# Second chunks of x2 turned by DMA in planes of 16-bit halves

## The chip, the cores and the metric

One core of one Trainium2 chip runs the whole program in one launch. The metric is the device time of an execution in microseconds. The kernel before takes 731.89 us, the median of three executions (731.84 to 732.41).

## The reference, cut to what matters

Four batches of 448 positions and 768 channels go through sigmoid attention, a gated convolution block and a token and channel mixer. The stretch that matters here is the output projection and the token mixing behind it:

```
x  = attn(q, k, v)                       # (4, 448, 768)
g  = sigmoid(causal_conv5(x))
x2 = (g * (x @ w_val)) @ w_out           # the x2 of this document
u  = x2 + (relu(x2.T @ w_tok1) @ w_tok2).T
out = u + relu(u @ w_ch1) @ w_ch2
```

`x2` is computed with its channels on the partitions (x2.T), and `x2.T @ w_tok1` contracts over positions, so it needs x2 with positions on the partitions: each 128 x 448 chunk has to be turned over.

## The kernel before, in words

Weights and inputs are kept as pairs of a rounded high part and a low remainder, and each product is three matmuls (high x high, low x high, high x low). The work runs in stages: attention for all batches, then for each batch `b` the steps that `dense_steps(b)` hands back, then the channel mixer (`ch1`, `ch2`), which is two thirds of the time that is left.

The steps of a batch are called on TensorE in a list order written by hand. `val` holds six value projections (`proj(0, j)`, 18 matmuls each), whose result VectorE multiplies into the gate (L343) and splits into a high and a low part (L86 on ScalarE, L92 on VectorE). `outs` holds six output projections (`proj(1, j)`, 18 matmuls each, j is the chunk of 128 channels), whose result ScalarE copies to `x2T[j]` (L348), the transposes of the chunks (`transp(j)`, four 128 x 128 transposes on TensorE, L357, with a high part by ScalarE, L359, and a low part by VectorE, L360 and L361), and the token mixer: `tok1(half, t)` (11 matmuls of 384 columns, L374, needs three chunks of one half) and `tok2(j)` (6 matmuls, L387, whose sum VectorE adds to `x2T`, L391, and POOL stores). The second half's `tok1` and its `tok2` are called within the next batch's `val`, as `back1` and `back2`. The last 64 positions of a chunk are held twice (L349), so that the fourth transpose has 128 columns.

Beside these steps other work is woven in by `weave`, which calls a list of small operations in proportion to the matmuls passed. Within `outs` of batch b it is the convolution of batch b+1 (`post_ops`): six items, each of five passes of VectorE (L302 and four of L304), a high part by ScalarE (L309), a low part by VectorE (L312), a sigmoid by ScalarE (L315), and the load of a later item (`x_back`). Within `val` of batches 1 and 2 it is the decoding of three channel-mixer weights (`ch_ops`, `decode_ops`): six pieces `raw` of 768 KB are loaded by the SP queue (`ld_ch`), worked on by six passes of VectorE and two of ScalarE, and stored again by POOL (`keep`, L602). There are two buffers `raw`, and the load of piece n+2 is called behind the eighth operation of piece n:

```
                if k == 7:
                    load(n + 2)
```

Each engine and each queue works through its own instructions strictly in the order in which the program calls them. PSUM tiles of these steps come from one pool of six.

Of the kernel before, what the change touches and what calls it, by code (L numbers as in the profile page):

```python
# [30 lines left out]
def tile_kernel(ctx, tc, qT, kT, v, w_val, conv_w, w_out, w_tok1, w_tok2, w_ch1, w_ch2, out):  # L31
# [130 lines left out]
    dn = {}  # L162
    pd = {}

    wt1H = wts.tile([P, NF + 1, NTOK], F32R, name="wt1H")
# [153 lines left out]
    def dense_steps(b):  # L319
        gv, x2T, x2, h1 = {}, {}, {}, {}  # L320
        cur = {}

        def proj(sel, j, part):
# [16 lines left out]
            if sel == 0:  # L340
                g = gate_t.pop(b * NP + j)

                nc.vector.tensor_tensor(out=g, in0=ps[:, :S], in1=g, op=ALU.mult)  # L343
                gv[j] = mid.tile([P, 2, S], F32R, tag="g", bufs=6, name="gv")
                split(gv[j][:, 0], gv[j][:, 1], g)
            else:
                x2T[j] = dn["late"].tile([P, 512], F32, tag="x2T", bufs=KD, name="x2T")
                nc.scalar.activation(out=x2T[j][:, :S], in_=ps[:, :S], func=AF.Copy)  # L348
                nc.vector.tensor_copy(x2T[j][:, S:], x2T[j][:, R0:S])  # L349

        def transp(j):
            half, jj = divmod(j, KH)
            if jj == 0:
                x2[half] = dn["late"].tile([P, 2 * NF + 1, HALF], F32R, tag="x2", bufs=1, name="x2")
            pt = pd["pool"].tile([P, NF + 1, P], F32, tag="d", bufs=pd["n"], name="pst")
            for c in range(NF + 1):
                nc.tensor.transpose(pt[:, c], x2T[j][:, c * P : (c + 1) * P], ident)  # L357
            x = x2[half][:, :, jj * P : (jj + 1) * P]
            nc.scalar.activation(out=x[:, : NF + 1], in_=pt, func=AF.Copy)  # L359
            nc.vector.tensor_tensor(out=x[:, NF + 1 :], in0=pt[:, :NF], in1=f(x[:, :NF]), op=ALU.subtract)  # L360
            nc.vector.tensor_tensor(  # L361
                out=x[REM:, NF], in0=pt[REM:, NF], in1=f(x[REM:, NF]), op=ALU.subtract
            )

# [51 lines left out]
        if b == 0:  # L416

            first[2:4] = first[3], first[2]
        outs = first + tr(0) + pj(1, 2) + tr(1) + pj(1, 3) + tr(2) + pj(1, 4)
        outs += t1(0, 0) + t1(0, 1) + pj(1, 5) + tr(3) + t2(0) + tr(4) + t2(1) + tr(5) + t2(2)  # L420
        return val, outs, t1(1, 0) + t1(1, 1), t2(3) + t2(4) + t2(5)

# [152 lines left out]
    def ld_ch(pool, fc, which):  # L575
        raw = pool.tile([P, 2 * DC], I32, tag="raw", bufs=2, name="raw")
        if which == 0:
# [47 lines left out]
    def ch_ops(pool, pieces):  # L625
# [5 lines left out]

        load(0)
        load(1)
        ops = []
        for n in range(len(pieces)):
            cur = []

            def op(k, n=n, cur=cur):
# [3 lines left out]
                if k == 7:  # L642
                    load(n + 2)

# [60 lines left out]
    with tc.manual_schedule():  # L705
# [23 lines left out]
        for b in range(B):  # L729
# [4 lines left out]
            else:  # L734
# [101 lines left out]
```

## Time and profile before

| | |
|---|---|
| median of three executions | 731.89 us |
| the profiled execution | 731.72 us, span 729.8 us |
| TensorE busy | 724.2 us of the span (99%) |
| VectorE busy | 398.9 us (55%) |
| ScalarE busy | 256.7 us (35%) |
| POOL busy | 40.2 us (6%) |
| granted clock of TensorE | full in all 40 slices |
| transposes of x2 (L357) | 96 in 24 groups of four |

The page gives first each engine's busy time, then its share in 40 equal slices, then the DMA queues, the chain of waits that ended last, and groups of instructions. The three stretches from one batch's first output projection to the next one's are alike; a stretch of time is read best from the timeline, which lists an engine's instructions in order with the idle time ahead of each.

### The profile page before, as it was taken

To read this page: it belongs to the slowest core of one execution; us is meant where nothing else is said; L and a number is where in the kernel's file an instruction comes from. 1 tells how busy PE (TensorE), PEld (TensorE's weight loads), DVE (VectorE), ACT (ScalarE), POOL (GpSimd) and SP (SyncE) were. 2 spreads that over 40 slices of the span, in tenths; PEclk is the share of its full clock that TensorE was granted. 3 is DMA by queue.
4 is the path that set the end of the run, shared out by engine and by line. 5 is a ranking of instruction groups with operands and counts; after the bars stand their busy time and mean duration, and the time that the engine had idled before them with its cause. 6 is when DMAs were issued, how large, how long until landed. Compare 5 with 4: busy or idle time off the path is not lost.

```text
span 729.8 us, 10824 instructions
## 1 busy us (share of the span) xinstructions
PE 724.2 (99%) x4360; PEld 594.1 (81%) x4360; DVE 398.9 (55%) x690; ACT 256.7 (35%) x379; POOL 40.2 (6%) x90
## 2 busy tenths in 40 slices
PE   8999999999999999999999999999999999999998
PEld 3344444799999999999998888888888899999997
DVE  1899766489889878965577999320100400040002
ACT  6899888344334333422343434200000200020000
POOL 0001100000111111002012000000000000000000
PEclk9999999999999999999999999999999999999999
DMA  9847997221344232044927453250000610042001
GB/s 298 252 153 236 266 299 234 83 91 47 102 150 147 76 127 101 17 147 131 311 82 227 162 172 127 67 172 0 1 0 1 201 38 0 1 128 67 1 1 65
DMA packets 56737, 87.24 MB, mean 120 GB/s; under 512 B 8032, under 2 KB 48240, under 8 KB 56688
## 3 DMA queue, kind: packets, MB, share of 16 engines
q1 hardware_dynamic: 50352, 62.86, 28.1%
q0 software_dynamic: 5904, 23.23, 9.0%
q8 instruction: 34, 0.56, 0.3%
q10 hardware_dynamic: 432, 0.46, 0.2%
q14 instruction: 15, 0.12, 0.1%
HBM read 66.68 MB, written 19.86 MB: 119 GB/s over the span
## 4 chain that ended last, share of the span: by engine, by line
PE 98%; ACT 1%; DVE 1%; issue 0%; ACTq 0%
PE psd L334 24%; PE psh L674 24%; PE pso L695 24%; PE pss L256 8%; PE psy L271 8%; PE pst L374 4%; PE pst L387 4%; PE pst L357 1%; ACT ga L258 1%; PE psi L718 0%; DVE dec_a L123 0%; DVE w L132 0%; ACT dec_a L111 0%; DVE dec_e L129 0%; DVE ur L701 0%
## 5 line engine op out<-in xcount | busy, mean ns | idle before, releaser
L88 DVE SCALAR_TENSOR_TENSOR r<-psh,r 128x384 fp32r<-128x384 f32 (+1 forms) x47 | 29.3, 623 | 213.4 <-ACT r L86 213.4
L674 PE MATMUL psh<-us,wch 128*128 128x512 f32 (+1 forms) x648 | 135.5, 362 | 0.0
L695 PE MATMUL pso<-r,wch 128*128 128x384 f32 (+1 forms) x630 | 131.1, 361 | 0.0
L674 PEld LDWEIGHTS psh<-us,wch 128*128 128x128 f32 x648 | 117.3, 188 | 12.7
L695 PEld LDWEIGHTS pso<-r,wch 128*128 128x128 f32 x630 | 113.8, 188 | 11.9
L86 ACT ACTIVATE r<-psh 128x384 fp32r<-128x384 f32 (+1 forms) x47 | 25.5, 543 | 230.7 <-PE psh L674 230.6
L334 PE MATMUL psd<-gv,wo 128*128 128x448 f32 x432 | 92.3, 369 | 0.0
L258 ACT ACTIVATE ga<-pss,bias_s 128x896 f32<-128x896 f32 x84 | 83.6, 1005 | 19.0 <-PE pss L256 18.2
L334 PE MATMUL psd<-xs,w 128*128 128x448 f32 x432 | 89.9, 367 | 0.0
L334 PEld LDWEIGHTS psd<-xs,w 128*128 128x128 f32 x432 | 80.9, 188 | 8.2 <-issue 0.7
L334 PEld LDWEIGHTS psd<-gv,wo 128*128 128x128 f32 x432 | 80.2, 188 | 6.6
L256 PE MATMUL pss<-q,k 64*64 64x448 f32 x672 | 78.5, 537 | 1.0 <-ACT ga L258 0.9
L271 PE MATMUL psy<-ga,v 64*64 64x448 f32 x672 | 77.6, 536 | 0.0
L304 DVE SCALAR_TENSOR_TENSOR gate<-xb,cw,gate 128x448 f32<-128x448 f32 x96 | 65.7, 685 | 2.8
L256 PEld LDWEIGHTS pss<-q,k 64*64 64x64 f32 x672 | 26.0, 133 | 39.4 <-issue 29.0
L271 PEld LDWEIGHTS psy<-ga,v 64*64 64x64 f32 x672 | 25.7, 133 | 37.4 <-issue 35.9
L111 ACT ACTIVATE dec_a<-dec_a,exp_b 128x768 int32<-128x768 int32 (+3 forms) x43 | 36.8, 868 | 37.1 <-DVE dec_a L108 37.1
L123 DVE SCALAR_TENSOR_TENSOR dec_a<-raw,dec_a 128x768 int32<-128x768 int32 (+2 forms) x42 | 37.3, 888 | 19.7 <-ACT dec_a L111 19.7
L674 PE MATMUL psh<-us,w 128*128 128x512 f32 (+1 forms) x216 | 45.2, 362 | 0.0
L695 PE MATMUL pso<-r,w 128*128 128x512 f32 (+1 forms) x216 | 45.1, 362 | 0.0
L674 PEld LDWEIGHTS psh<-us,w 128*128 128x128 f32 x216 | 39.1, 188 | 4.3
L695 PEld LDWEIGHTS pso<-r,w 128*128 128x128 f32 x216 | 39.1, 188 | 4.2
(80 smaller groups left out, 648.7 us busy)
## 6 DMA issues: line engine op xcount, KB each, us to landing
raw<-w_ch SPq DMA_DIRECT2D x24, 768.0 KB, 4.4
v<-v SPq DMA_DIRECT2D x24, 224.0 KB, 6.5
uscr<-x2T POOLq DMA_DIRECT2D x24, 224.0 KB, 3.7
q<-qT SPq DMA_DIRECT2D x23, 224.0 KB, 4.3
k<-kT SPq DMA_DIRECT2D x22, 224.0 KB, 4.5
raw<-w_out POOLq DMA_DIRECT2D x6, 768.0 KB, 8.4
wscr<-pre POOLq DMA_DIRECT2D x12, 384.0 KB, 3.6
xscr<-xb SPq DMA_DIRECT2D x18, 224.0 KB, 4.7
```

What stands on the lines that cost most here:

```text
L88: nc.vector.scalar_tensor_tensor(out=l_out, in0=src, scalar=0.0, in1=f(h_out), op0=ALU.max, op1=ALU.subtract)
L111: nc.scalar.activation(out=t["a"], in_=t["a"], func=AF.Relu, scale=8.0, bias=exp_b)
L123: nc.vector.scalar_tensor_tensor(out=t["a"], in0=hi, scalar=-0x80000000, in1=t["a"], op0=ALU.bitwise_and, op1=ALU.bitwise_or)
L256: nc.tensor.matmul(ps[cols, j, :S], k[rows, keys], q[rows], start=True, stop=True)
L258: nc.scalar.activation(out=a, in_=ps[:, :, :S], func=AF.Sigmoid, bias=bias_s, scale=QK_SCALE)
L271: nc.tensor.matmul(y_t[i + h][cols, :S], v_t[i][rows, c, cols], a[rows, j], start=c == 0, stop=c == NB - 1)
L304: nc.vector.scalar_tensor_tensor(out=acc, in0=x[:, t : t + S], scalar=w, in1=acc, op0=ALU.mult, op1=ALU.add)
L334: nc.tensor.matmul(ps[:, :S], w(a, kk), s[:, c, :], start=kk == 0 and n == 0, stop=kk == KD - 1 and n == 2,)
L374: nc.tensor.matmul(ps[:, :HALF], a, x[:, m], start=n == 0, stop=n == len(mm) - 1)
L387: nc.tensor.matmul(ps[:, :S], a, m[:, t, :], start=t == 0 and n == 0, stop=t == KT - 1 and n == 2)
L674: nc.tensor.matmul(ps[:, :n_t], wch[fc][0][a][:, kk * P : (kk + 1) * P], us_t[t, kk][:, c, :], start=kk == 0 and n == 0, stop=kk == KD - 1 ...
L695: nc.tensor.matmul(acc[j][:, :n_t], wch[fc][1][a][:, j * P : (j + 1) * P], r[c], start=fc == 0 and n == 0, stop=fc == KF - 1 and n == 2,)
```

## The change

In batches 0, 1 and 2 the chunks 0, 2 and 4 no longer go to TensorE. Behind the copy of `x2T[j]` ScalarE writes the low and the high 16 bits of each word into two planes (`planes`: one pass over 2 x 448 halves, one over the 2 x 64 that are held twice), and the SP queue turns the 128 x 1024 halves by one DMA transpose into `planesT`. Later (`joined`) ScalarE puts the halves together into words (one pass over 1024 halves), writes the high part (one pass over 512 words), and VectorE the low part in two passes, as before. `planes`, `planesT` and `word` have one buffer each. VectorE's copy of the 64 positions (L349) falls away for these chunks.

The list of `outs` is written in another order for batches 0 to 2: the first joining stands behind projection 2, the second behind projection 4, and `tok1` of the first half behind projection 5 where it stood behind projection 4. The decoding of the stored weights has one buffer `raw` where it had two, so the load of piece n+1 is called behind the eighth operation of piece n.

```diff
@@ dense_steps
                 x2T[j] = dn["late"].tile([P, 512], F32, tag="x2T", bufs=KD, name="x2T")
                 nc.scalar.activation(out=x2T[j][:, :S], in_=ps[:, :S], func=AF.Copy)
-                nc.vector.tensor_copy(x2T[j][:, S:], x2T[j][:, R0:S])
+                if by_dma(j):
+                    planes(j)
+                else:
+                    nc.vector.tensor_copy(x2T[j][:, S:], x2T[j][:, R0:S])
+        def by_dma(j):
+            return b + 1 < B and j % 2 == 0
...
+        def planes(j):
+            p = tp["pool"].tile([P, 2, 512], U16, tag="planes", bufs=1, name="planes")
+            w = x2T[j].bitcast(U16).rearrange("p (n t) -> p t n", t=2)
+            nc.scalar.activation(out=p[:, :, :S], in_=w[:, :, :S], func=AF.Copy)
+            nc.scalar.activation(out=p[:, :, S:], in_=w[:, :, R0:S], func=AF.Copy)
+            pt = tp["pool"].tile([P, 2, NF + 1, P], U16, tag="planesT", bufs=1, name="planesT")
+            nc.sync.dma_start_transpose(pt.rearrange("p t c d -> p (t c) d"), p.rearrange("p t n -> p (t n)"))
+            pl[j] = pt
+        def joined(j):
...
+            w = tp["pool"].tile([P, NF + 1, P], F32, tag="word", bufs=1, name="word")
+            nc.scalar.activation(
+                out=w.rearrange("p c d -> p (c d)").bitcast(U16).rearrange("p (n t) -> p t n", t=2),
+                in_=pl.pop(j).rearrange("p t c d -> p t (c d)"), func=AF.Copy,
+            )
+            x = x2[half][:, :, jj * P : (jj + 1) * P]
+            nc.scalar.activation(out=x[:, : NF + 1], in_=w, func=AF.Copy)
+            nc.vector.tensor_tensor(out=x[:, NF + 1 :], in0=w[:, :NF], in1=f(x[:, :NF]), op=ALU.subtract)
+            nc.vector.tensor_tensor(
+                out=x[REM:, NF], in0=w[REM:, NF], in1=f(x[REM:, NF]), op=ALU.subtract
+            )
...
+        def jn(j):
+            return [(0, lambda: joined(j))]
...
-        outs = first + tr(0) + pj(1, 2) + tr(1) + pj(1, 3) + tr(2) + pj(1, 4)
-        outs += t1(0, 0) + t1(0, 1) + pj(1, 5) + tr(3) + t2(0) + tr(4) + t2(1) + tr(5) + t2(2)
+        if b + 1 < B:
+            tr0, tr2, tr4 = jn(0), jn(2), jn(4)
+        outs = first + pj(1, 2) + tr0 + tr(1) + pj(1, 3) + pj(1, 4) + tr2 + pj(1, 5) + t1(0, 0) + t1(0, 1)
+        outs += tr(3) + tr4 + t2(0) + t2(1) + tr(5) + t2(2)
@@ ld_ch
-        raw = pool.tile([P, 2 * DC], I32, tag="raw", bufs=2, name="raw")
+        raw = pool.tile([P, 2 * DC], I32, tag="raw", bufs=1 if fc in PRE else 2, name="raw")
@@ ch_ops
-        load(0)
-        load(1)
+        held = 1 if pieces[0][0] in PRE else 2
+        for n in range(held):
+            load(n)
...
                 if k == 7:
-                    load(n + 2)
+                    load(n + held)
```

The changed program's order shows three places. The first is ScalarE in `outs` of batch 1, around projections 1 to 4. Names: `xs` is an item's high part, `gate` its sigmoid, `x_...` the turned chunk's high part. Before:

```order
L348 ACTIVATE x2T<-psd 128x448
L315 ACTIVATE gate<-gate 128x448
L359 ACTIVATE x_2408<-pst 128x4x128
L309 ACTIVATE xs<-xb 128x448
L348 ACTIVATE x2T<-psd 128x448
L315 ACTIVATE gate<-gate 128x448
L359 ACTIVATE x_2408<-pst 128x4x128
L309 ACTIVATE xs<-xb 128x448
L348 ACTIVATE x2T<-psd 128x448
```

Now, from the copy of chunk 2:

```order
L350 ACTIVATE x2T<-psd 128x448
L378 ACTIVATE planes<-x2T 128x2x448
L379 ACTIVATE planes<-x2T 128x2x64
L317 ACTIVATE gate<-gate 128x448
L389 ACTIVATE word<-planesT 128x2x512
L394 ACTIVATE x_2454<-word 128x4x128
L368 ACTIVATE x_2454<-pst 128x4x128
L311 ACTIVATE xs<-xb 128x448
L350 ACTIVATE x2T<-psd 128x448
```

The first joining (L389, L394, of chunk 0) stands behind the planes of chunk 2, and the high part of chunk 1 (L368) behind both.

The second place is VectorE in the same stretch, up to the low part of the last chunk that `tok1` waits for. Before, from the low part of chunk 1 to that of chunk 2:

```order
L360 TENSOR_TENSOR x_2408<-pst,x_2408 128x3x128
L361 TENSOR_TENSOR x_2408<-pst,x_2408 64x128
L304 SCALAR_TENSOR_TENSOR gate<-xb,cw,gate 128x448 x2
L312 TENSOR_TENSOR xs<-xb,xs 128x448
L302 TENSOR_SCALAR gate<-xb,cw 128x448
L304 SCALAR_TENSOR_TENSOR gate<-xb,cw,gate 128x448
L349 COPY x2T<-x2T 128x64
L304 SCALAR_TENSOR_TENSOR gate<-xb,cw,gate 128x448
L360 TENSOR_TENSOR x_2408<-pst,x_2408 128x3x128
```

Now, from the low part of chunk 1 (L369, L370), which follows that of chunk 0 (L395, L396) at once, to that of chunk 2 (the last row):

```order
L369 TENSOR_TENSOR x_2454<-pst,x_2454 128x3x128
L370 TENSOR_TENSOR x_2454<-pst,x_2454 64x128
L306 SCALAR_TENSOR_TENSOR gate<-xb,cw,gate 128x448 x2
L314 TENSOR_TENSOR xs<-xb,xs 128x448
L304 TENSOR_SCALAR gate<-xb,cw 128x448
L306 SCALAR_TENSOR_TENSOR gate<-xb,cw,gate 128x448
L354 COPY x2T<-x2T 128x64
L306 SCALAR_TENSOR_TENSOR gate<-xb,cw,gate 128x448 x3
L314 TENSOR_TENSOR xs<-xb,xs 128x448
L304 TENSOR_SCALAR gate<-xb,cw 128x448
L306 SCALAR_TENSOR_TENSOR gate<-xb,cw,gate 128x448 x2
L395 TENSOR_TENSOR x_2454<-word,x_2454 128x3x128
```

Between the low parts of chunks 1 and 2 stood six passes and a copy of VectorE; now it is eleven passes and a copy.

The third place is VectorE behind that, up to the low parts of `tok1`'s two results (`h_...`), which `tok2` waits for. Now:

```order
L396 TENSOR_TENSOR x_2454<-word,x_2454 64x128
L306 SCALAR_TENSOR_TENSOR gate<-xb,cw,gate 128x448 x2
L314 TENSOR_TENSOR xs<-xb,xs 128x448
L354 COPY x2T<-x2T 128x64
L304 TENSOR_SCALAR gate<-xb,cw 128x448
L306 SCALAR_TENSOR_TENSOR gate<-xb,cw,gate 128x448
L89 SCALAR_TENSOR_TENSOR h_2592<-pst_2580,h_2592 128x384
L306 SCALAR_TENSOR_TENSOR gate<-xb,cw,gate 128x448 x2
L89 SCALAR_TENSOR_TENSOR h_2610<-pst_2598,h_2610 128x384
```

Before it read:

```order
L361 TENSOR_TENSOR x_2408<-pst,x_2408 64x128
L304 SCALAR_TENSOR_TENSOR gate<-xb,cw,gate 128x448 x2
L312 TENSOR_TENSOR xs<-xb,xs 128x448
L302 TENSOR_SCALAR gate<-xb,cw 128x448
L349 COPY x2T<-x2T 128x64
L304 SCALAR_TENSOR_TENSOR gate<-xb,cw,gate 128x448 x2
L88 SCALAR_TENSOR_TENSOR h_2548<-pst_2536,h_2548 128x384
L304 SCALAR_TENSOR_TENSOR gate<-xb,cw,gate 128x448 x2
L88 SCALAR_TENSOR_TENSOR h_2566<-pst_2554,h_2566 128x384
```

The passes between the last low part and those of `tok1`'s results are nearly the same as before; all of them stand one convolution item further back.

## Rows read from the trace of the kernel before

**Rows 1.** The page, part 1: busy us, share, instructions.

```profile
PE 724.2 (99%) x4360; PEld 594.1 (81%) x4360; DVE 398.9 (55%) x690; ACT 256.7 (35%) x379; POOL 40.2 (6%) x90
```

**Rows 2.** Windows, batches 1 and 0: us, busy us of PE PEld DVE ACT POOL, clock.

```profile
216.74:278.75 62.01, 62.01 (x321) 57.36 (x320) 52.35 (x95) 22.62 (x40) 7.70 (x18) 1.00 0.33 109
...
154.72:216.74 62.02, 62.02 (x322) 57.27 (x321) 53.41 (x97) 24.28 (x43) 4.88 (x13) 1.00 0.34 110
```

**Rows 3.** Timeline, TensorE, batch 1: start, us, line, what, count.

```profile
278.75 7.60 PE L334 MATMUL psd<-gv,wo 128*128 128x448 f32 x36
286.19 0.60 PE L357 MATMUL pst<-ident,x2T 128*128 128x128 f32 x4
...
290.28 0.60 PE L357 MATMUL pst<-ident,x2T 128*128 128x128 f32 x4
...
298.45 0.34 PE L374 MATMUL pst<-x,wt1H 128*128 128x384 f32 x1
...
302.29 3.87 PE L334 MATMUL psd<-gv,wo 128*128 128x448 f32 x18
```

**Rows 4.** Timeline, ScalarE, the same batch.

```profile
282.67 0.55 ACT L348 ACTIVATE x2T<-psd 128x448 f32<-128x448 f32 x1 [4.58 <-PE psd L334]
...
290.92 0.57 ACT L315 ACTIVATE gate<-gate 128x448 f32<-128x448 f32 x1
291.39 0.59 ACT L359 ACTIVATE x<-pst 128x512 fp32r<-128x512 f32 x1
```

**Rows 5.** Groups by line, shapes apart, ScalarE: busy us, mean ns | idle.

```profile
L111 ACT ACTIVATE dec_a<-dec_a,exp_b 128x768 int32<-128x768 int32 x36 | 33.7, 936 | 37.1 <-DVE dec_a L108 37.1
...
L111 ACT ACTIVATE dec_a<-dec_a,exp_b 128x256 int32<-128x256 int32 x4 | 2.0, 498 | 0.0
```

**Rows 6.** Timeline, VectorE, the same batch.

```profile
276.92 0.63 DVE L92 TENSOR_TENSOR gv<-gate,gv 128x448 fp32r<-128x448 f32 x1 [0.65 <-ACT gv L86]
...
280.40 0.45 DVE L302 TENSOR_SCALAR gate<-xb,cw 128x448 f32<-128x448 f32 x1
280.88 1.40 DVE L304 SCALAR_TENSOR_TENSOR gate<-xb,cw,gate 128x448 f32<-128x448 f32 x2
...
287.93 0.56 DVE L360 TENSOR_TENSOR x<-pst,x 128x384 fp32r<-128x384 f32 x1
288.50 0.29 DVE L361 TENSOR_TENSOR x<-pst,x 64x128 fp32r<-64x128 f32 x1
288.82 0.68 DVE L304 SCALAR_TENSOR_TENSOR gate<-xb,cw,gate 128x448 f32<-128x448 f32 x1
289.43 0.62 DVE L312 TENSOR_TENSOR xs<-xb,xs 128x448 fp32r<-128x448 f32 x1
289.96 0.45 DVE L302 TENSOR_SCALAR gate<-xb,cw 128x448 f32<-128x448 f32 x1
```

**Rows 7.** Timeline, VectorE, batch 0: its first convolution pass.

```profile
158.79 0.45 DVE L302 TENSOR_SCALAR gate<-xb,cw 128x448 f32<-128x448 f32 x1
```

**Rows 8.** Timeline, VectorE, value projections of batch 1: pieces' last and first passes.

```profile
196.56 0.96 DVE L132 SCALAR_TENSOR_TENSOR pre<-raw,dec_e 128x768 fp32r<-128x768 f32 x1
...
200.15 0.55 DVE L108 TENSOR_SCALAR dec_a<-raw 128x768 int32<-128x768 int32 x1
...
205.47 0.96 DVE L132 SCALAR_TENSOR_TENSOR pre<-raw,dec_e 128x768 fp32r<-128x768 f32 x1
...
208.35 0.56 DVE L108 TENSOR_SCALAR dec_a<-raw 128x768 int32<-128x768 int32 x1
209.49 0.62 DVE L343 TENSOR_TENSOR gate<-psd,gate 128x448 f32<-128x448 f32 x1 [0.59 <-PE psd L334]
```

**Rows 9.** DMA issues from 160 to 330 us: count, KB each, us to landing.

```profile
raw<-w_ch SPq DMA_DIRECT2D x6, 768.0 KB, 5.2
...
xb<-xscr SPq DMA_DIRECT2D x14, 224.0 KB, 2.5
```

**Rows 10.** DMA issues of the whole span: the slowest kind.

```profile
w<-wscr POOLq DMA_DIRECT2D x8, 384.0 KB, 8.9
```

More of the change, by code (lines that the diff above doesn't have):

```diff
@@ L13 @@
 U32 = mybir.dt.uint32
+U16 = mybir.dt.uint16
 AF = mybir.ActivationFunctionType
@@ L163, in tile_kernel @@
     pd = {}
+    tp = {}
     wt1H = wts.tile([P, NF + 1, NTOK], F32R, name="wt1H")
@@ L319, in dense_steps @@
     def dense_steps(b):
-        gv, x2T, x2, h1 = {}, {}, {}, {}
+        gv, x2T, x2, h1, pl = {}, {}, {}, {}, {}
         cur = {}
@@ L348, in proj @@
                 nc.scalar.activation(out=x2T[j][:, :S], in_=ps[:, :S], func=AF.Copy)
-                nc.vector.tensor_copy(x2T[j][:, S:], x2T[j][:, R0:S])
+                if by_dma(j):
[4 more added lines that the diff above has]
+            return b + 1 < B and j % 2 == 0
         def transp(j):
             half, jj = divmod(j, KH)
-            if jj == 0:
+            if half not in x2:
                 x2[half] = dn["late"].tile([P, 2 * NF + 1, HALF], F32R, tag="x2", bufs=1, name="x2")
@@ L362, in transp @@
                 out=x[REM:, NF], in0=pt[REM:, NF], in1=f(x[REM:, NF]), op=ALU.subtract
+            )
[8 more added lines that the diff above has]
+        def joined(j):
+            half, jj = divmod(j, KH)
+            if half not in x2:
+                x2[half] = dn["late"].tile([P, 2 * NF + 1, HALF], F32R, tag="x2", bufs=1, name="x2")
+            w = tp["pool"].tile([P, NF + 1, P], F32, tag="word", bufs=1, name="word")
[8 more added lines that the diff above has]
+                out=x[REM:, NF], in0=w[REM:, NF], in1=f(x[REM:, NF]), op=ALU.subtract
             )
@@ L741, in tile_kernel @@
                 dn["late"] = tc.alloc_tile_pool(name="late", bufs=1, side="right", reuse_waits="tile")
+                tp["pool"] = tc.alloc_tile_pool(name="tp", bufs=1, side="left")
                 pre = tc.alloc_tile_pool(name="pre", bufs=1, side="left")
@@ L751, in tile_kernel @@
                 pre.release()
+                tp["pool"].release()
                 xbp.release()
```

## The prediction

> **What bounds the kernel now.** I read the page's busy times first: TensorE is busy for 99% of the span, no other engine above 55% [rows 1]. So time can only be won by taking matmuls away, and anything that makes TensorE wait is lost in full. The windows then show that each stretch from one batch's first output projection to the next one's takes 62.0 us, with TensorE busy throughout at full clock, and VectorE busy for 52 to 53 us of it [rows 2]. VectorE is thus the next engine in line, and its idle time is not spread evenly: within `outs` it runs almost without a gap. The timelines give the pace of each kind of step, and the order shows what stands behind what.
>
> **What is removed.** In TensorE's timeline two projections of 18 take 286.19 - 278.75 = 7.44 us, 3.72 each, or 0.207 a matmul; a projection with a group of four transposes takes 290.28 - 286.19 = 4.09, so the group costs 0.37; two `tok1` take 302.29 - 298.45 = 3.84, 1.92 each and 0.175 a matmul [rows 3]. Three groups a batch go, in three batches: 9 x 0.37 = **-3.3 us**. That is all that can be won.
>
> **What is added on ScalarE.** No row shows a pass over 16-bit elements. The nearest are the integer passes: 0.936 us for 768 elements, 0.498 for 256, so 0.86 ns an element [rows 5]. That gives 1.05 us for 896 halves, 0.39 for 128 and 1.16 for 1024; a next pass starts about 0.1 before the end of one it doesn't need (0.57 long, 0.47 apart [rows 4]). As bounds I take half of that, if halves go at twice the pace, and 1.6 times, if the step of two halves costs more. ScalarE has the time for it (24 of 62 us [rows 2]); the place matters. Times from here on run from a batch's first output projection.
>
> Projection 2 ends at 3 x 3.72 = 11.16. The copy `x2T` starts 0.20 later (282.47 to 282.67) and takes 0.55 [rows 3, 4]: 11.9. Planes of chunk 2: 13.25. A sigmoid: 13.7. Only then does the joining of chunk 0 stand in ScalarE's queue: the word to 14.8, the high part (0.59 [rows 4]) to **15.4**.
>
> **Who waits for that.** VectorE's queue has chunk 0's low part behind two items of convolution and half a third. An item takes 3.75: L302 0.48, four L304 at 0.71 (0.61 if the next doesn't need it), L312 0.53 [rows 6]. In batch 0 it begins at 158.79 - 154.72 = 4.07 [rows 2, 7] and reaches that low part at 13.5, so VectorE stands still until 15.4. From there to the last low part that `tok1` needs (chunk 2) the order has (L306, L314, L354, L395 and the like are lines of the changed kernel, for L304, L312, L349, L360): two low parts, 2 x 0.90 (L360 0.57, L361 0.33 apart), two L306 1.33, L314 0.53, L304 0.48, L306 0.61, a copy 0.1, three L306 2.04, L314 0.53, L304 0.48, two L306 1.33 [rows 6]. The sum is 9.2: it starts at 24.6 and ends at 25.15. ScalarE has its high part long before that: copy 4 ends at 18.96 + 0.36 + 0.75 = 19.7, planes 21.1, word 22.2, high part 22.8.
>
> TensorE wants it at the third matmul of `tok1`: six projections 22.32, one group of transposes 0.37, two matmuls 0.35: 23.05. It waits **2.1 us**. Then the rest of `tok1` (28.7), a group of transposes (29.1) and four matmuls of `tok2` bring it to 29.9, where it needs the low part of `tok1`'s second result. VectorE has in between L396 0.33, two L306 1.33, L314 0.53, a copy 0.1, L304 0.48, L306 0.61, L89 0.47, two L306 1.33, L89 0.56 (L360 taken for L89 [rows 6]): 25.15 + 5.75 = 30.9. It waits **1.05 us** more. A batch is then 62.0 - 1.1 + 2.1 + 1.05 = 64.05, that is **+6.1 us** over three, with the -3.3 in it.
>
> **One buffer raw.** The load of the next piece can go out only when VectorE's last pass on this one has ended; 768 KB land after 5.2 us [rows 9]. VectorE came to the next piece 200.15 - 197.52 = 2.6 us later at the first border and 208.35 - 206.43 = 1.9 at the second [rows 8]. It will stand 2.6 and 3.3 us there, less 0.6 that it waited for TensorE anyway [rows 8]: 5.3 late at the end of `val`, in batches 1 and 2. The low part of the last gated value ended at 277.55, 1.2 ahead of `outs` [rows 3, 6], and now ends at 4.1; projection 0 needs it at 17 x 0.207 = 3.5. So 4.7 is covered and 0.6 is lost. Item 0 began at 1.65 [rows 3, 6] and now at 6.95; the 64-position copy of chunk 1, behind it and half of item 1, is done at 12.6, and the one group of transposes wants it at 11.16 + 0.6: 0.85 lost. VectorE comes to the joining at 16.3, 0.3 behind the word, while TensorE's need at `tok1` lies 0.85 later, so 0.55 of the wait of 2.1 is used up: +0.9, twice, **+1.8**. If loads land in 4.2 the cover holds and this is nothing; at 6.4 it is 2 to 3 us a batch.
>
> **The transposing DMA.** No row shows one. Its 256 KB lie between 2.5 us (224 KB by the same queue [rows 9]) and 8.9 (the slowest kind [rows 10]). I take the load's 5.2, since the two share the queue. What does a duration T cost? Chunk 0's planes are done at 3.72 + 0.75 + 1.35 = 5.9; its transfer must free the one buffer `planes` before chunk 2's passes, and chunk 2's transfer must wait for the first word (1.35 + 0.45 + 1.15), then planes of chunk 4, word, high part, low part (3.8): 12.65 + 2T. That passes 25.15 only from T = 6.2 on. Below it the transfer costs nothing; above, 2 us a batch for each us of T. At 8.9: 30.45, 5.3 later, +16 us in all. In the SP queue the loads of items behind a transposing transfer wait with it; they are wanted some 10 us later and land in 2.5 [rows 9].
>
> The Trainium skill speaks against the change here: VectorE: DVE Perf Modes, section The three transpose paths, has 1.3 us for 128 x 128 through the crossbar against 0.39 on TensorE, and its table sends a transpose to TensorE where PSUM will do. Eight such blocks one after another would be 10.5 us (an estimate from that page), and by the formula +25.5 us more, 765 us. Advanced Engine Details and Errata, section X-Bar Transpose (TRN2), has such transfers as fast as plain ones, and by that T stays off the path. No run so far shows which.
>
> **Sum.** 731.72 (profiled execution) + 6.1 + 1.8 = 739.6. That execution lies 0.17 under the median, so 739.8 is compared with 731.89. A difference of 0.2% (1.5 us) is about what can be told from none.
>
> **The rivals.**
> - **Long transfers.** Above T = 6.2 the two transfers in a row set the end, each with the loads of `raw` ahead of it in the queue in batches 1 and 2. For it: large transfers there take 5.2 to 8.9. Against: plain ones of this size take 2.5. With T from 7 to 9: 744 to 756. Chance 0.25. The skill's 1.3 us a block, named above, would be its far end.
> - **Cheap halves.** If the 16-bit passes take half the time, the joining comes 1.25 earlier and the wait of 2.1 falls to 0.85: +0.8 a batch, 734, and up to 738 with VectorE's lateness from `raw`. Against: durations in ScalarE's rows go by elements. Chance 0.05.
> - **The join doesn't hold VectorE up** (the other side). It decides at chunk 0's high part: were it there by 13.2 instead of 15.4, chunk 2's own high part, 22.8, would be last and its low part done by 23.4; `tok1` and `tok2` would wait 0.35 and 1.05, against 1.1 won: +0.3 a batch, 732.6, no change. If those two are covered too, -3.3: 728.4. It takes passes at a third of the rows' pace and loads within 2.6 us. Chance 0.10, half for each.
>
> That the transposes stay where they were is excluded: the built order has nine groups fewer.
>
> **Numbers.** My forecast, 736 to 743, has 0.60. Faster by over 0.2%: 0.05; within: 0.05; slower: 0.90. The range goes from cheap halves, 734, to long transfers of 8.9, 755.
>
> **What would show it.** Right: TensorE's stretches of 64 to 65 us; waits of about 2 us ahead of the third matmul of the first `tok1`, put down to VectorE, and of 1 us in the first `tok2`; VectorE idle at L395 on ScalarE's L394 in batch 0, and idle at L109 on the load in `val`. Transposing transfers that land in under 6 us. Wrong: TensorE waits put down to ScalarE or to `planesT` (long transfers), or none at `tok1` at all.

## The result, and the profile after

The changed kernel takes **742.16 us** (median of 4 runs, 741.75 to 742.65). The kernel before, run beside it, takes 732.15 (731.84 to 732.77). The ratio is 1.0136, with a 95% interval of 1.0123 to 1.0148. The forecast was 739.8, some 8 us slower; measured are 10 us. The profiled execution has a span of 740.0 us, against 729.8 before.

The page of the kernel after, busy times and chain of waits:

```profile
PE 724.9 (98%) x4324; PEld 591.4 (80%) x4324; DVE 397.2 (54%) x681; ACT 278.3 (38%) x406; POOL 40.4 (5%) x90
...
PE 85%; DVE 8%; ACT 3%; DMA 2%; issue 1%; SPq 0%; DVEq 0%; ACTq 0%
```

TensorE has 36 instructions fewer than in [rows 1]. The chain that ended last now runs for 15% of the span through other engines, DMA and issue, where it was 2% before. The windows show where, cut at the first output projection of batches 0, 1 and 2 (us; busy us of PE, PEld, DVE, ACT, POOL; granted clock):

```profile
154.68:218.84 64.16, 61.27 (x309) 56.01 (x308) 48.68 (x87) 29.54 (x49) 4.86 (x13) 1.00 0.36 107
218.84:283.95 65.11, 61.91 (x310) 55.81 (x309) 51.42 (x92) 29.96 (x49) 7.89 (x18) 1.00 0.42 128
283.95:350.08 66.13, 63.55 (x310) 57.37 (x308) 52.90 (x93) 29.24 (x49) 5.33 (x11) 0.97 0.33 97
```

Against 62.0 for such a stretch before [rows 2], the three are 2.1, 3.1 and 4.1 longer: 9.3 in all. The remaining 0.9 of the span lies behind TensorE's last group of matmuls, which began at 719.93 and now begins at 729.23. From its start to the end of the span it was 9.9 before and is 10.8 now. The last six output transfers land later there; the DMA issues of that end, before (723 to 730 us) and after (732 to 740 us; count, KB each, us to landing):

```profile
out<-ur SPq DMA_DIRECT2D x6, 192.0 KB, 1.9
...
out<-ur SPq DMA_DIRECT2D x6, 192.0 KB, 2.8
```

This comes with the change. The four profiles without transposing transfers (before, experiments 1, 2 and 8) have 9.85 to 9.9 us and a landing time of 1.9; the eight with them have 10.4 to 10.8 us and 2.5 to 2.8. No run shows why.

TensorE's timeline of the kernel after, batches 0 and 1 (in brackets the idle time before the instruction, and what ended it; L409 is the first token-mixing product `tok1`, L422 the second, `tok2`, L366 the transposes):

```profile
177.83 0.44 PE L409 MATMUL pst<-x,wt1H 128*128 128x384 f32 x1 [0.67 <-ACT x L394]
...
179.81 0.61 PE L409 MATMUL pst<-x,wt1H 128*128 128x384 f32 x2 [1.36 <-DVE x L395]
...
185.66 0.47 PE L422 MATMUL pst<-wt2H,h 128*128 128x448 f32 x1 [0.86 <-DVE h L89]
...
231.23 0.33 PE L366 MATMUL pst<-ident,x2T 128*128 128x128 f32 x1 [0.53 <-DVE x2T L354]
...
242.96 0.45 PE L409 MATMUL pst<-x,wt1H 128*128 128x384 f32 x1 [0.46 <-ACT x L394]
...
244.93 0.62 PE L409 MATMUL pst<-x,wt1H 128*128 128x384 f32 x2 [1.34 <-DVE x L395]
```

In batch 0 the first `tok1` waits twice, 2.03 together, and the first `tok2` once, 0.86. Batch 1 has the same three (the one at `tok2` is 0.87) and one at the transposes of chunk 1. The first wait is for the high part of chunk 2 (ScalarE, L394), the second for its low part (VectorE, L395). VectorE's timeline in batch 0 shows why the low part is late:

```profile
169.98 0.56 DVE L395 TENSOR_TENSOR x<-word,x 128x384 fp32r<-128x384 f32 x1 [1.79 <-ACT x L394]
...
179.20 0.55 DVE L395 TENSOR_TENSOR x<-word,x 128x384 fp32r<-128x384 f32 x1
```

VectorE stands still for 1.79 us until ScalarE has joined chunk 0, works without a gap from there on, and comes to chunk 2 at 179.20. ScalarE's groups show what the joining costs (busy us, mean ns of one | idle; L378 and L379 make the halves, L389 joins them, L394 makes the high part):

```profile
L389 ACT ACTIVATE word<-planesT 128x1024 uint16<-128x1024 uint16 x9 | 12.3, 1364 | 0.0
L378 ACT ACTIVATE planes<-x2T 128x896 uint16<-128x896 uint16 x9 | 8.6, 952 | 0.6 <-DMA planesT<-planes 0.3
L394 ACT ACTIVATE x<-word 128x512 fp32r<-128x512 f32 x9 | 5.7, 632 | 0.3
...
L379 ACT ACTIVATE planes<-x2T 128x128 uint16<-128x128 uint16 x9 | 2.6, 294 | 0.0
```

The waits of VectorE by what it waited for, over the whole kernel (us in total, times, longest), two rows of after and one of before:

```profile
DVE dec_a L109 <- DMA raw<-w_ch: 18.3, 6, 4.9
...
DVE x L395 <- ACT x L394: 5.5, 6, 1.8
```

```profile
DVE dec_a L108 <- DMA raw<-w_ch: 5.6, 2, 4.8
```

The first row is the single `raw` buffer, the last the same wait before; the four that are new stand in the value projections of batches 1 and 2, 2.6 to 3.0 each. The transposing transfers, which no row of before showed, took this from issue to landing:

```profile
DMA to landing us min/median/max: 3.0/3.2/6.3
```

The one of 6.3 is the first of batch 1. A `raw` load of 768 KB went out at 224.45, just ahead of it (224.88), and ScalarE stands 0.33 for it at the next chunk's halves.

In its third batch the kernel also loses time without waiting. TensorE's timeline of batch 2, and windows of two us each behind the last of these waits:

```profile
287.45 8.43 PE L336 MATMUL psd<-gv,wo 128*128 128x448 f32 x39 [0.24 <-ACT gv L87]
...
308.46 0.44 PE L409 MATMUL pst<-x,wt1H 128*128 128x384 f32 x1 [0.46 <-ACT x L394]
...
310.43 0.62 PE L409 MATMUL pst<-x,wt1H 128*128 128x384 f32 x2 [1.35 <-DVE x L395]
```

```profile
310.00:312.00 2.00, 1.57 (x8) 1.57 (x9) 1.90 (x4) 0.00 (x0) 0.00 (x0) 0.90 0.12 23
312.00:314.00 2.00, 2.00 (x8) 2.00 (x7) 1.93 (x6) 0.95 (x2) 0.00 (x0) 0.50 0.00 0
314.00:316.00 2.00, 2.00 (x13) 1.97 (x11) 1.73 (x3) 0.22 (x1) 0.00 (x0) 0.75 0.00 0
```

From 310.43 on TensorE is busy throughout, but at a granted clock of 0.50, the lower of its two levels (1.2 GHz), for part of that time. Over the six us the mean is 0.72, so 1.7 us are lost. `tok2` no longer waits in this batch. Neither batch 0 nor batch 1 shows such a fall, nor any stretch of this kind before.

### The profile page after: what moved, and what is told of

Same layout as the page of the kernel before. It is cut to its first block, busy times and chain, and to the rows that moved or that the text cites. A ratio compares the mean times of both kernels' runs of the same rounds, so it can differ in the third digit from the quotient of the medians.

```text
span 740.0 us, 10775 instructions
## 1 busy us (share of the span) xinstructions
PE 724.9 (98%) x4324; PEld 591.4 (80%) x4324; DVE 397.2 (54%) x681; ACT 278.3 (38%) x406; POOL 40.4 (5%) x90
## 4 chain that ended last, share of the span: by engine, by line
PE 85%; DVE 8%; ACT 3%; DMA 2%; issue 1%; SPq 0%; DVEq 0%; ACTq 0%
PE psh L715 23%; PE pso L736 23%; PE psd L336 16%; PE pss L258 8%; PE psy L273 8%; PE pst L422 3%; DVE gate L306 3%; PE pst L409 3%; DMA raw<-w_ch 1%; ACT word L389 1%; ACT ga L260 1%; PE pst L366 1%; DVE xs L314 1%; DVE dec_a L124 0%; DMA k<-kT 0%
## 5 line engine op out<-in xcount | busy, mean ns | idle before, releaser
L715 PEld LDWEIGHTS psh<-us,wch 128*128 128x128 f32 x648 | 117.3, 188 | 12.6
L336 PE MATMUL psd<-gv,wo 128*128 128x448 f32 x432 | 90.8, 368 | 0.2 <-ACT gv L87 0.2
L124 DVE SCALAR_TENSOR_TENSOR dec_a<-raw,dec_a 128x768 int32<-128x768 int32 (+2 forms) x42 | 37.3, 888 | 19.7 <-ACT dec_a L112 19.6
```

Of the source, the lines that this page charges most:

```text
L124: nc.vector.scalar_tensor_tensor(out=t["a"], in0=hi, scalar=-0x80000000, in1=t["a"], op0=ALU.bitwise_and, op1=ALU.bitwise_or)
L336: nc.tensor.matmul(ps[:, :S], w(a, kk), s[:, c, :], start=kk == 0 and n == 0, stop=kk == KD - 1 and n == 2,)
L715: nc.tensor.matmul(ps[:, :n_t], wch[fc][0][a][:, kk * P : (kk + 1) * P], us_t[t, kk][:, c, :], start=kk == 0 and n == 0, stop=kk == KD - 1 ...
```

## The experiments

Theory: three things add up. Nine groups of transposes are gone (-3.3 us); ScalarE's joining stands late in an in-order queue, VectorE waits there, and so `tok1` and `tok2` wait (some 3 us a batch); the single `raw` buffer makes VectorE late in batches 1 and 2. Rivals: the transposing transfer itself sets the end; the 16-bit passes are too long wherever they stand; the new order of the work alone is to blame.

All kernels in one table. The stretches are from one batch's first output projection to the next one's, read from each profile; the kernel before, beside them, had medians of 732.14 (1 to 4), 732.41 (5 to 8) and 732.39 (9, 10).

| kernel | batch 0, 1, 2 (us) | median us | ratio to before, 95% interval |
|---|---|---|---|
| before | 62.0, 62.0, 62.0 | 732.15 | |
| changed kernel | 64.2, 65.1, 66.1 | 742.16 | 1.0136 (1.0123 to 1.0148) |
| 1 single raw buffer alone | 62.0, 64.1, 64.4 | 737.03 | 1.0068 (1.0056 to 1.0081) |
| 2 order alone | 62.6, 62.0, 62.0 | 733.12 | 1.0015 (1.0006 to 1.0025) |
| 3 transfers doubled | 66.3, 68.5, 67.5 | 750.02 | 1.0245 (1.0231 to 1.0259) |
| 4 two raw buffers again | 64.4, 64.7, 64.4 | 740.89 | 1.0122 (1.0108 to 1.0136) |
| 5 joining earlier | 62.7, 64.8, 64.9 | 739.51 | 1.0098 (1.0082 to 1.0113) |
| 6 reordered, one raw | 61.5, 64.3, 64.4 | 738.32 | 1.0078 (1.0064 to 1.0092) |
| 7 reordered, two raw | 61.6, 63.2, 60.8 | 732.43 | 0.9998 (0.9990 to 1.0007) |
| 8 that order, TensorE transposes | 62.6, 62.1, 62.1 | 733.04 | 1.0010 (1.0001 to 1.0018) |
| 9 as 7, one load later | 61.1, 60.9, 60.9 | 729.90 | **0.9968 (0.9956 to 0.9980)** |
| 10 as 3, two buffers of planes | 64.2, 66.9, 65.9 | 744.97 | 1.0170 (1.0156 to 1.0184) |

### 1. The single raw buffer alone

```diff
-        raw = pool.tile([P, 2 * DC], I32, tag="raw", bufs=2, name="raw")
+        raw = pool.tile([P, 2 * DC], I32, tag="raw", bufs=1 if fc in PRE else 2, name="raw")
...
-        load(0)
-        load(1)
+        held = 1 if pieces[0][0] in PRE else 2
+        for n in range(held):
+            load(n)
...
-                    load(n + 2)
+                    load(n + held)
```

> Change: the kernel before with one change taken over, the single raw buffer (one instead of two) for the two pieces of each projection that are decoded in the second half of a batch; transposes, order of the output work and joining stay as before. Theory (three costs side by side: waits at the first token-mixing products +6, the single buffer +2 to +4, transposes gone -3.3): 1.8 to 4 us slower than before, 734 to 736, with waits of TensorE at projection 0 and the transposes of chunk 0 of batches 1 and 2 and almost none in batch 0. Rival 'the joining is all of it': within 0.7 us of before. Rival 'the buffer is most of it': 7 us or more slower.

4.9 us slower: more than the theory's upper end, less than the rival. VectorE's and TensorE's timelines of this kernel in batch 1 (L360 is the low part of a chunk here):

```profile
203.30 0.56 DVE L108 TENSOR_SCALAR dec_a<-raw 128x768 int32<-128x768 int32 x1 [2.36 <-DMA raw<-w_ch]
...
214.09 0.56 DVE L108 TENSOR_SCALAR dec_a<-raw 128x768 int32<-128x768 int32 x1 [2.70 <-DMA raw<-w_ch]
```

```profile
225.78 0.33 PE L357 MATMUL pst<-ident,x2T 128*128 128x128 f32 x1 [0.40 <-DVE x2T L349]
...
239.28 0.62 PE L374 MATMUL pst<-x,wt1H 128*128 128x384 f32 x2 [0.94 <-DVE x L360]
```

VectorE loses 5.1 us at the two borders, near the forecast's 2.6 and 3.3. But without the joining it is still late at the first `tok1`, and TensorE waits 0.94 there, which the theory had not counted for this kernel. Batches 1 and 2 get 2.1 and 2.3 longer; batch 0 stays.

### 2. The new order alone

```diff
-            if jj == 0:
+            if half not in x2:
...
-        outs = first + tr(0) + pj(1, 2) + tr(1) + pj(1, 3) + tr(2) + pj(1, 4)
-        outs += t1(0, 0) + t1(0, 1) + pj(1, 5) + tr(3) + t2(0) + tr(4) + t2(1) + tr(5) + t2(2)
+        outs = first + pj(1, 2) + tr(0) + tr(1) + pj(1, 3) + pj(1, 4) + tr(2) + pj(1, 5) + t1(0, 0) + t1(0, 1)
+        outs += tr(3) + tr(4) + t2(0) + t2(1) + tr(5) + t2(2)
```

> Change: the kernel before with only the new order of the output work in the first three batches (chunk 0 turned over after output projection 2, chunk 2 after projection 4 and projection 5 ahead of the first token-mixing products); all chunks turned over by TensorE, two raw buffers. Theory: the order by itself costs nothing, within 0.5 us of before, since TensorE's own transposes are ready 2 us after they are begun. Rival 'the order of the work, and not the way by DMA, makes the token-mixing products wait': 3 us or more slower, with waits at the third product of the first token-mixing pair and the first product of the second pair.

1.0 us slower, twice the theory's bound. TensorE's groups of `tok1` and `tok2` in this kernel (busy us, mean ns | idle before):

```profile
L374 PE MATMUL pst<-x,wt1H 128*128 128x384 f32 x112 | 29.8, 335 | 0.0
L387 PE MATMUL pst<-wt2H,h 128*128 128x448 f32 x96 | 28.2, 374 | 0.6 <-DVE h L88 0.6
```

Batch 0 has one wait of 0.57 in `tok2` for VectorE's L88; batches 1 and 2 have none at all. In the profile the first output projection of batch 0 also begins 0.9 later than before (155.6 for 154.7), ahead of all that the edit touches; over all the profiles this start lies between 154.7 and 156.3. `tok1` waits nowhere. The rival falls: the order makes `tok1` wait only with the way by DMA.

### 3. Transfers doubled

```diff
-            nc.sync.dma_start_transpose(pt.rearrange("p t c d -> p (t c) d"), p.rearrange("p t n -> p (t n)"))
+            for _ in range(2):
+                nc.sync.dma_start_transpose(pt.rearrange("p t c d -> p (t c) d"), p.rearrange("p t n -> p (t n)"))
```

> Change: the changed kernel with each transposing transfer issued twice to the same tile, so that its planes land about 3.2 us later (some 6.4 instead of 3.2 after the first issue). Theory (the end is set by the in-order joining passes on ScalarE and VectorE behind a fixed place in the program, and the transfers have slack): 0 to 2.5 us slower than the changed kernel, 742 to 745. Rival 'the transfer's length is on the path': each of the three transfers of a batch, or at least the two ahead of the first token-mixing pair, pushes what follows by 3.2, so 9 (three batches by 3.2) to 19 us slower than the changed kernel, 751 to 761.

7.9 us slower than the changed kernel: between the two, and so both missed. TensorE's timeline and windows of this kernel, batch 0:

```profile
181.71 0.45 PE L410 MATMUL pst<-x,wt1H 128*128 128x384 f32 x1 [2.93 <-ACT x L395]
...
182.84 0.91 PE L410 MATMUL pst<-x,wt1H 128*128 128x384 f32 x2 [0.52 <-DVE x L396]
```

```profile
182.00:184.00 2.00, 1.49 (x6) 1.16 (x6) 1.90 (x5) 1.02 (x3) 0.00 (x0) 0.74 0.86 223
184.00:186.00 2.00, 2.00 (x8) 2.00 (x7) 1.97 (x5) 0.00 (x0) 0.10 (x1) 0.50 0.24 48
186.00:188.00 2.00, 2.00 (x11) 1.97 (x11) 1.68 (x4) 0.96 (x2) 0.00 (x0) 0.90 0.88 200
```

TensorE's idle time in that stretch is 2.93 + 0.52 = 3.45, only 0.56 more than the changed kernel's 2.89: the waits at `tok1` grew by 1.42, and the 0.86 at `tok2` is gone. But the batch is 2.1 longer, since the granted clock falls right behind the wait: its mean over these six us is 0.71, 1.7 us lost. All three batches show such a fall. The wait itself comes by ScalarE:

```profile
169.44 0.95 ACT L378 ACTIVATE planes<-x2T 128x896 uint16<-128x896 uint16 x1 [1.46 <-DMA planesT<-planes]
...
178.61 0.95 ACT L378 ACTIVATE planes<-x2T 128x896 uint16<-128x896 uint16 x1 [0.91 <-DMA planesT<-planes]
```

It stands at the next chunk's halves until the transfer has read the one buffer `planes`, and the joining is queued behind. Experiment 10 takes that up.

### 4. Two raw buffers again

```diff
-        raw = pool.tile([P, 2 * DC], I32, tag="raw", bufs=1 if fc in PRE else 2, name="raw")
+        raw = pool.tile([P, 2 * DC], I32, tag="raw", bufs=2, name="raw")
...
-            to = [pool.tile([P, DM], F32R, tag=f"pre{a}", bufs=1, name="pre") for a in range(2)]
+            to = [pool.tile([P, DM], F32R, tag="pre0", bufs=1, name="pre"), raw[:, :DM].bitcast(F32R)]
...
-        held = 1 if pieces[0][0] in PRE else 2
+        held = 2
...
-                if k == 7:
+                if k == (8 if pieces[n][0] in PRE else 7):
```

> Change: the changed kernel with two raw buffers again for the pieces that had one (the low part of such a piece is written into the second half of its own raw tile to make room, and the next load but one waits for the piece's last copy). Theory: 1.5 to 3 us faster than the changed kernel, 739 to 740.5; the waits at projection 0 and at the transposes of batches 1 and 2 are gone, those at the token-mixing products stay (about 2 us and 0.9 us in each of three batches). Rival 'the buffer is most of it': 6 us or more faster, so at or below before. Rival 'the buffer costs nothing': within 0.7 us of the changed kernel.

1.3 us faster than the changed kernel, under the 1.5 expected. The three batches are now alike, 64.4 to 64.7, with the three waits of batch 0 in each; those at projection 0 and at the transposes are gone. What remains is the joining: about 3.5 a batch over experiment 9, which waits nowhere. TensorE's and VectorE's timelines of this kernel, batch 1:

```profile
243.40 0.44 PE L409 MATMUL pst<-x,wt1H 128*128 128x384 f32 x1 [0.94 <-ACT x L394]
...
245.38 0.62 PE L409 MATMUL pst<-x,wt1H 128*128 128x384 f32 x2 [1.37 <-DVE x L395]
```

```profile
235.56 0.56 DVE L395 TENSOR_TENSOR x<-word,x 128x384 fp32r<-128x384 f32 x1 [3.74 <-ACT x L394]
```

The buffer alone costs 4.9, and with the joining there only 1.3. VectorE's wait shows why. Here it stands 3.74 us in batch 1 until ScalarE has joined chunk 0; in the changed kernel, where the buffer has made it late, it stands 0.24 at that place:

```profile
235.10 0.56 DVE L395 TENSOR_TENSOR x<-word,x 128x384 fp32r<-128x384 f32 x1 [0.24 <-ACT x L394]
```

What it loses to the buffer it would have lost to the joining. TensorE's wait for ScalarE differs by less: it is 0.94 in batch 1 here, but 0.65 and 0.66 in batches 0 and 2, and in batch 1 a transposing transfer behind a `raw` load holds ScalarE up by 0.33.

### 5. Joining earlier

```diff
-        outs = first + pj(1, 2) + tr0 + tr(1) + pj(1, 3) + pj(1, 4) + tr2 + pj(1, 5) + t1(0, 0) + t1(0, 1)
+        p2, p4 = pj(1, 2), pj(1, 4)
+        outs = first + p2[:2] + tr0 + p2[2:] + tr(1) + pj(1, 3) + p4[:2] + tr2 + p4[2:] + pj(1, 5) + t1(0, 0) + t1(0, 1)
```

> Change: the changed kernel with the joining of chunks 0 and 2 called one third of a projection earlier (ahead of the last part of output projections 2 and 4 instead of behind it), all else as it is, one raw buffer. Theory (joining is late because it stands late in the in-order queues of ScalarE and VectorE): the two waits at the third product of the first token-mixing pair (0.67 and 1.36 in batch 0) all but vanish; what VectorE then has late is the halves of the first pair's own result, and the wait at the second pair grows from 0.86 to about 1.2 to 2.5; 1.5 to 4.5 us faster than the changed kernel in all, 737.5 to 740.5. Rival 'the passes are too long for the stretch, wherever they stand': within 1 us of the changed kernel, the waits only moved. Rival 'the transfer is late': the joining waits at ScalarE for the planes (over 1 us in each batch), and nothing is won.

2.7 us faster than the changed kernel, as the theory has it. `tok1` no longer waits, and `tok2` waits twice; TensorE's timeline of this kernel, batch 1:

```profile
247.82 0.47 PE L422 MATMUL pst<-wt2H,h 128*128 128x448 f32 x1 [1.12 <-DVE h L89]
...
249.60 0.47 PE L422 MATMUL pst<-wt2H,h 128*128 128x448 f32 x1 [0.91 <-DVE h L89]
```

A place in the order a third of a projection earlier thus turned 2.9 us of waits at both products into 1.6 to 2.0 at the second, and batch 0 is 1.4 shorter. ScalarE does stand at the joining of chunk 0 until the transfer has landed, 1.05 us in batch 0 and 1.04 in batch 1, as the rival of the late transfer had it; that it wins nothing is refuted.

### 6 to 8. Another order, with one and with two raw buffers, and its control

```diff
-        outs = first + pj(1, 2) + tr0 + tr(1) + pj(1, 3) + pj(1, 4) + tr2 + pj(1, 5) + t1(0, 0) + t1(0, 1)
-        outs += tr(3) + tr4 + t2(0) + t2(1) + tr(5) + t2(2)
+        p2, p4, p5 = pj(1, 2), pj(1, 4), pj(1, 5)
+        outs = first + p2[:2] + tr0 + p2[2:] + pj(1, 3) + p4[:1] + tr(1) + p4[1:2] + tr2 + p4[2:]
+        outs += p5[:2] + t1(0, 0) + t1(0, 1) + p5[2:] + tr(3) + t2(0) + tr4 + t2(1) + tr(5) + t2(2)
```

Experiment 7 has the edit of experiment 4 besides; experiment 8 puts this order into the kernel before, with `tr(0)`, `tr(2)` and `tr(4)` for the joinings.

> Change: the changed kernel with the output work of the first three batches in another order (joining of chunks 0 and 2 earlier, chunk 1's transposes after the first third of projection 4, the first token-mixing pair ahead of the last third of projection 5, the joining of chunk 4 behind the first product pair of chunk 0); the single raw buffer stays. Theory: batch 0, which the buffer doesn't touch, takes about 61 us from its first output projection to the next one's, a little less than before (62.0); batches 1 and 2 keep the buffer's cost and take 63 to 65; the whole 734 to 738. Rival 'the passes are too long for the stretch': batch 0 takes over 63 as well and the whole is 740 or more.

> Change: the same order of the output work as in the run with one raw buffer, with two raw buffers again. Theory (the three costs are all there is): the waits are gone and what is left is the gain of the nine groups of transposes, each of the three batches 61 us instead of 62.0: 728.5 to 730, 2 to 3.5 us faster than before. Rival 'the halves by DMA and ScalarE cost more than TensorE's transposes wherever they stand': 733 or more. Rival 'the order pays, not the way by DMA': as fast as the same order with TensorE's transposes, within 0.7 us.

> Change: the kernel before with the same new order of the output work, all chunks turned over by TensorE, two raw buffers. It is the control for that order. Theory: the order without the way by DMA wins nothing, within 0.7 us of before (731.5 to 732.9), each batch 62.0 us. Rival 'the order pays by itself': 2 us or more faster than before.

In experiment 6 batch 0 falls to 61.5, though the passes and the transfers are the same: "the passes are too long for the stretch" falls. Its median, 738.3, is just over the theory's range, with `tok1` waiting for VectorE 1.8 in batches 1 and 2. The profiled execution, 737.0 at a mean granted clock of 1.000, lies in it; the three others, 738.0 to 738.8, have 0.995 to 0.998. In experiment 7 batch 2 takes 60.8, but batch 1 takes 63.2, and the whole is as fast as before: the expectation failed on one batch. The control, 733.0, wins nothing by its order. By the medians the third rival could stand (0.6 apart), but the stretches speak against it: batch 2 takes 62.1 in the control and 60.8 here. SP's, ScalarE's and TensorE's timelines of experiment 7 in batch 1:

```profile
223.30 0.38 SPq L619 DMA_DIRECT2D raw<-w_ch  x1
223.78 1.24 SPq L381 DMA_TRANSPOSE planesT<-planes  x1
```

```profile
229.54 1.37 ACT L389 ACTIVATE word<-planesT 128x1024 uint16<-128x1024 uint16 x1 [3.31 <-DMA planesT<-planes]
```

```profile
240.60 0.62 PE L409 MATMUL pst<-x,wt1H 128*128 128x384 f32 x2 [1.56 <-DVE x L395]
```

The transposing transfer goes out right behind a load of 768 KB, lands some 5.7 us later, and ScalarE waits 3.31 for it; with no load just ahead it waits 1.03 in batch 0 and 0.51 in batch 2.

### 9. That load later

The edit is against experiment 7:

```diff
+                if k == 0 and n == 3:
+                    load(4)
                 if k == 0:
                     cur += ch_parts(pool, *pieces[n], raws.pop(n))
...
-                if k == (8 if pieces[n][0] in PRE else 7):
+                if k == (8 if pieces[n][0] in PRE else 7) and n != 2:
```

> Change: the reordered kernel with two raw buffers, with one raw load moved: the load of the fifth decoded piece, issued on SP at 223.3 in batch 1 just ahead of the first transposing transfer (which then landed at 229.5, 5.7 after its issue, and not 3.2 to 3.9 as in the other batches, and made the first token-mixing pair wait 1.56), is issued when the decoding of the fourth piece begins, in batch 2. Theory: batch 1 takes 61 to 61.6 us from its first output projection to the next one's instead of 63.24, and the whole is 1.3 to 2 us faster than with the load where it was: 730.3 to 731.2, or 1 to 2.3 us faster than before. Rival 'batch 1 was slow for another reason, or the load only collides elsewhere': within 0.5 us of the run without the move, as fast as before. Rival 'the way by DMA gives nothing even when nothing waits': all three batches at 61.5 or less, yet the whole not faster than before.

729.9 us, 2.5 faster than before and faster by more than its interval: the version that beats both, a little better than the theory's 730.3 to 731.2. The windows of its three batches, and then the group of `tok1` (busy us, mean ns | idle before):

```profile
156.03:217.15 61.12, 61.06 (x309) 56.07 (x308) 52.58 (x94) 31.69 (x52) 4.89 (x13) 1.00 0.40 125
217.15:278.01 60.86, 60.86 (x310) 56.17 (x309) 51.94 (x92) 30.08 (x49) 7.73 (x18) 1.00 0.39 124
278.01:338.86 60.85, 60.85 (x310) 56.17 (x308) 48.30 (x86) 27.56 (x46) 5.35 (x11) 1.00 0.37 105
```

```profile
L409 PE MATMUL pst<-x,wt1H 128*128 128x384 f32 x112 | 29.8, 335 | 0.0
```

TensorE waits nowhere. The three stretches sum to 182.8 against 186.05 before: the nine groups of transposes were worth 3.2 us. The control with TensorE's transposes (experiment 8) was not run with this load moved. It has only one wait, 0.38 in batch 0, so the load could win little there; it takes 733.04.

### 10. Transfers doubled, two buffers of planes

The edit is against experiment 3:

```diff
-            p = tp["pool"].tile([P, 2, 512], U16, tag="planes", bufs=1, name="planes")
+            p = tp["pool"].tile([P, 2, 512], U16, tag="planes", bufs=2, name="planes")
```

> Change: the kernel with every transposing transfer issued twice (750.0 us), with two buffers for planes instead of one, so that ScalarE may fill the next planes while a transfer still reads the last. Theory (with the transfer doubled ScalarE stood at the next chunk's planes until the transfer had read the one buffer, 0.9 to 1.5 us each time, with the joining of the chunk before queued behind it, and the waits of TensorE, near 3 us in a row, then brought its clock down to 0.5 for 3 us in each batch): the waits of ScalarE at planes go over to the joining, which now starts when the transfer lands, about 1.2 us earlier for chunk 2; the wait at the third product of the first pair falls from 2.6 to 4 us to about 1.5 to 3, and the whole by 2 to 6 us, to 744 to 748. Rival 'the joining waits for the transfer itself, the buffer adds nothing': within 1 us of 750.0.

5.0 us faster than experiment 3, as the theory has it. ScalarE no longer waits at the halves, and TensorE's timeline in batch 0 is that of the changed kernel:

```profile
178.98 0.44 PE L410 MATMUL pst<-x,wt1H 128*128 128x384 f32 x1 [0.67 <-ACT x L395]
...
180.94 0.61 PE L410 MATMUL pst<-x,wt1H 128*128 128x384 f32 x2 [1.35 <-DVE x L396]
```

The same waits, 64.2 us, with transfers twice as long: in the order of the changed kernel the transfer is not on the path in that batch. In batch 1 it is: with a `raw` load ahead of the first transfer ScalarE waits 1.11 at the joining, and TensorE 1.44 at the first matmul of `tok1`, for 0.46 in the changed kernel. Batches 1 and 2 are 66.9 and 65.9; in both the clock falls to 0.50 to 0.58 behind the waits of `tok1`.

## Why the prediction was right, and where it was off

**Direction and mechanism: right.** TensorE is idle 2.9 us in batch 0, at the places named, on the engine named for most of it. From the batch's start, VectorE stands until 15.3 (169.98 - 154.68; forecast 15.4), comes to chunk 2's low part at 24.5 (24.6), and TensorE goes on with `tok1` at 25.1 (25.15) and with `tok2` at 31.0 (30.9).

**Transposes removed, -3.3:** right, 3.2 in experiment 9.

**Waits at `tok1` and `tok2`, 3.15 a batch:** nearly right. Batch 0 came to 64.16 where 64.05 was forecast. The step that was off is "ScalarE has its high part long before that". It was held against VectorE's need, at 24.6. But TensorE wants the high part too, for the first matmul of `tok1` at 22.7 (six projections and a group of transposes), and has it only at 177.8 - 154.7 = 23.1, against 22.8 forecast. So 0.46 to 0.67 of the wait is put down to ScalarE and not to VectorE. The prediction had named such a wait as a sign of long transfers; it isn't one in batch 0, where ScalarE never waits for a transfer. The term that was mis-sized is the joining pass: 1.36 us for 1024 halves, taken as 1.16. The pass that makes 896 halves took 0.95, taken as 1.05. So halves are not cheap, and that rival falls. (In the sum for copy 4 the 18.96 holds the 0.36 already: 19.7 is 18.60 + 0.36 + 0.75.)

**One buffer raw, +0.9 in batches 1 and 2:** right in kind, too large in size, and its parts didn't come out as forecast. Against experiment 4, which differs by the buffer alone, batch 1 is 0.45 longer (65.11 to 64.66), half of what was forecast. Its parts were all smaller: no wait at projection 0 where 0.6 was forecast (0.24 in batch 2), 0.53 at the transposes for 0.85, and the waits at `tok1` 0.2 shorter than in batch 0, where 0.55 was to be used up. That batch 1 is 0.95 longer than batch 0, as the +0.9 would have it, is in part luck. Batch 2 is 1.97 longer than batch 0, and there a term was missing: the clock. Its 1.7 us stand against 0.87 that `tok2` no longer waits. That one wait should swallow another was counted, and experiments 1 and 4 show it larger: 4.9 alone, 1.3 together.

**The transfer, no cost below 6.2 us:** right for the median of 3.2. In batch 1 one took 6.3, behind a load, and cost ScalarE 0.33. The formula itself was too low. With the transfers doubled (T = 6.3) it gives 12.65 + 12.6 = 25.25, 0.1 behind the 25.15 without; TensorE went on with `tok1` at 182.84 - 156.29 = 26.55, 1.4 later than in the changed kernel. Most of that is its first term: chunk 0's transfer goes out at 6.8 and not at 5.9, in SP's timeline of the changed kernel and in experiment 3 alike. In batch 0 the last third of projection 0 stands behind the first third of projection 1, so ScalarE copies chunk 0 later.

```profile
161.49 1.36 SPq L381 DMA_TRANSPOSE planesT<-planes  x1
```

In experiment 3 the clock took 1.7 more. Eight blocks one after another, by the Trainium skill's page VectorE: DVE Perf Modes, section The three transpose paths, would have been 10.5 us (an estimate from that page); all eight landed in 3.2 here, so that the measurement decides against that estimate. The Trainium skill's page Advanced Engine Details and Errata, section X-Bar Transpose (TRN2), has such transfers as fast as plain ones: the trace comes near it, with 3.2 us for 256 KB against 2.5 for 224 KB [rows 9], an eighth more for a KB.

**The range** held. Of the 10 us measured 8 were forecast. By the profiles batches 0 and 1 came out 0.1 and 0.15 over the forecast, batch 2 1.2 over it, most of it the clock, and 0.9 lies behind TensorE's last group. Neither the clock nor that end was in the prediction, so the time came near the range's upper end for reasons that the sum did not name. That "the join doesn't hold VectorE up" could be had was right as a mechanism, but not by shorter passes: it took another place in the order, two buffers and a load moved.

Why the clock fell in batch 2 and not in batch 1, whose waits at `tok1` are alike, stays open. It isn't the same in each execution of a kernel either: experiment 4 took 740.2 to 741.1 us at a mean granted clock of 1.000 in three executions and 742.3 at 0.993 in the fourth.

## What to carry to other kernels

Work that is moved off the engine that bounds a kernel pays only if its result is there when that engine comes to it: here the same passes and transfers cost 10 us in one order, and won 2.5 in another with two `raw` buffers and one load moved. A tile that finds its room by taking a double buffer away elsewhere pays with that buffer's hidden load: 4.9 us alone, 1.3 where the engine would have waited anyway. Count the place in each in-order queue, SP's too: a load of 768 KB ahead of a transfer of 256 KB brought its landing time from 3.2 to 5.5 us and more.

## What the runs showed that I had not expected

- A wait of TensorE can cost more than its length. Where it stood 2.9 us and then 0.5, the granted clock fell to 0.50 behind it, and about 1.7 us more were lost (experiment 3; the clock fell in all three batches). In the changed kernel it fell behind 0.46 and 1.35 us, in one batch of three.
- A transposing transfer of 256 KB lands after 3.2 us in the median, keeps SP's queue for 1.24 us at its issue, and lands after 5.5 to 6.3 when a 768 KB load is issued just ahead of it (batch 1 of the changed kernel and of experiments 4 to 7).
- The last output transfers, the same in all kernels, landed after 1.9 us without transposing transfers some 400 us ahead of them and after 2.5 to 2.8 with them. Why is open.
- Passes over 16-bit halves are not priced by their elements alone: joining 1024 halves into words took 1.36 us, 1.33 ns a half, making 896 halves from words 0.95, 1.06 ns a half. Between the two making passes (896 halves and 128, 0.29 us) each further half costs 0.86 ns, as an element does in [rows 5].
